# Sink-window attention by 64-query halves: 208 score columns per query, sinks inside the key slots

## The chip, the cores and the metric

One core of one Trainium2 chip runs the whole program. The metric is device time in microseconds for one execution. The engines that matter here are TensorE (matmuls and their weight loads), VectorE, ScalarE, GpSimd and SyncE, which only issues DMAs. Each engine works through its own queue in program order; a semaphore wait on one instruction holds up all that stand behind it on that engine.

## The reference

Input are q, k, v of shape (2, 8, 768, 64): two batches, eight heads, 768 positions, head width 64. Each query sees the keys of its own window (itself and the 127 before it) and the first `n_sink` keys (4 here, at most 16 in this path). Behind the attention come two feed-forward layers on 1536 tokens.

```
scores = q @ k^T / sqrt(64)
keep   = (key < n_sink) or (0 <= query - key < window)        # window = 128
a      = softmax(where(keep, scores, -1e9))
x      = (a @ v), heads side by side                          # 1536 x 512
x      = softplus(x @ w_in1) @ w_out1                         # 512 -> 2048 -> 512
out    = (h * clip(h + 3, 0, 6) / 6) @ w_out2,  h = x @ w_in2
```

## The kernel before

Attention works in groups: a group is one block of 128 queries with all eight heads, 12 groups (g = 0 to 11), six per batch; i = g mod 6 is the block within its batch. A half group n (0 to 23, two per group) is four heads. The loop at L623 runs over n and writes all engines' work in one fixed order, so that each engine's queue is the order of the text. `in_order` (L31) pins it: no planner moves anything within the attention.

For a half group, `scores` (L460 on in the text, matmul L483) multiplies q (64 rows of the head's width, 128 queries as weights) with 272 key columns: the block before and the own block, each in a slot of 128 keys and 8 sink columns of `ring`. The two heads of a pair lie in rows 0 to 63 and 64 to 127. Every head has a PSUM bank of its own. fp32 products show as two matmuls and two weight loads each. `exps` masks and takes the maximum on VectorE (L495), and the exponential with its sum on ScalarE (L500). `transposes` (L525) turns the probabilities, 128 x 128 at a time, by TensorE, and `copies` brings them from PSUM (L538 on VectorE, L540 on ScalarE). `apply_v` (L567) multiplies them with v, two blocks a head. The sinks' 16 columns go another way in blocks with i > 1: GpSimd collects the 64 sink columns of four heads (L505), one transpose (L516), one copy, and one product with the sinks' values, set up so that each head only meets its own (L552). Block i = 0 has 128 keys only, block i = 1 sees the sinks as ordinary keys.

Half n's second part (two heads) is transposed and applied in iteration n + 1, its first part transposed in iteration n and applied in n + 1. When a group's eight heads are complete, `normalise` (L581, VectorE) divides by the sum, `turn_x` (L589, TensorE) transposes the output, `store_hi` (L592, ScalarE) and `store_lo` (L596, VectorE) write it as a rounded part and its remainder; `store_lo` stands one iteration after `store_hi`.

Between, VectorE converts feed-forward weights (`Weights.half`, L96, L99, L102), then ScalarE (L106) and GpSimd (L107). `HALVES` (L26) says in which iterations: every odd one from 5 to 19, and each one from 20 to 23. DMA issues are on SyncE: `fetch` (q, k, v of a group, three groups ahead) and the weights.

The loop runs three iterations more than there are half groups. In the first two of these stand the first two products of the feed-forward part (`products`, L144, 12 matmuls each). Then the feed-forward part runs: `stage_a` (L144 and the activations L166 to L176), `stage_b` (L201), with the remaining 20 weight conversions under its first 16 steps.

Of the kernel before, what the change touches and what calls it, by code (L numbers as in the profile page):

```python
# [18 lines left out]
P = 128  # L19
NEG = 1.0e9  # L20
MAXSINK = 16
SK = MAXSINK // 2
SLOTW = P + SK
SLOTPOS = (0, 2, 1, 3)
# [343 lines left out]
def banded_attention(ctx, tc, qT_d, kT_d, v, ident, NSv, Wv, xT, psa, isq, w, ffn, flags):  # L368
# [8 lines left out]
    NS = 4 * MAXSINK  # L377
# [4 lines left out]
    pst = ctx.enter_context(tc.tile_pool(name="pst", bufs=2, space=PSUM))  # L382
    ps1 = ctx.enter_context(tc.tile_pool(name="ps1", bufs=1, space=PSUM))

    st = {}
    ring = one.tile([P, NP, 4, SLOTW], F32, name="ring")

    def fetch(g):
        b, i = divmod(g, NB)
        s = st.setdefault(g, {})  # L390
        s["q"] = thr.tile([P, NP, P], F32, tag="q", name=f"q_{g}")
        s["v"] = thr.tile([P, H, D], F32, tag="v", bufs=5, name=f"v_{g}")
        k = ring[:, :, SLOTPOS[g % 4], 0:P]

        for ps in (slice(0, NP),) if g else (slice(0, NP // 2), slice(NP // 2, NP)):
            for t, src, eng in ((s["q"], qT_d, nc.sync), (k, kT_d, nc.sync if g else nc.scalar)):
                src = src[b].rearrange("(p t) d s -> (t d) p s", t=2)[:, ps, i * P : (i + 1) * P]
                eng.dma_start(t[:, ps], src)
        nc.sync.dma_start(s["v"], v[b, i * P : (i + 1) * P])

    def fetch_sinks(b):

        t = two.tile([NS, H, D], F32, tag="vs", name=f"vs_{b}")
        rows = v[b, 0:MAXSINK].rearrange("m h d -> m (h d)")
        rows = bass.AP(rows.tensor, rows.offset, [[0, 4]] + [list(x) for x in rows.ap])
        nc.sync.dma_start(t.rearrange("p h d -> p (h d)"), rows)
        st["vs", b] = t

    def own_sinks(b):

        t = st["vs", b]
        nc.gpsimd.tensor_tensor(
            out=t, in0=t, in1=owner.rearrange("p (h o) -> p h o", o=1).to_broadcast([NS, H, D]), op=ALU.mult
        )
# [5 lines left out]
    wm = one.tile([P, 1], F32, name="wm")  # L420
    mA = one.tile([P, P], F32, name="mA")
    mB = one.tile([P, P], F32, name="mB")
    mS = one.tile([P, P], F32, name="mS")
    tB = one.tile([P, P], F32, name="tB")
    m_odd = one.tile([P, 2, SLOTW], F32, name="m_odd")
    m_even = one.tile([P, 2, SLOTW], F32, name="m_even")
    m_one = one.tile([P, 2, SLOTW], F32, name="m_one")
    m_zero = one.tile([P, P], F32, name="m_zero")
    ph = one.tile([NS, 2, 4], I32, name="ph")
    owner = one.tile([NS, H], F32, name="owner")  # L430

    def masks(i):

        if i == 0:
            nc.vector.tensor_scalar(out=mB, in0=rmc, scalar1=Wv, scalar2=hid, op0=ALU.is_ge, op1=ALU.mult)
            nc.vector.tensor_tensor(out=mB, in0=mB, in1=tB, op=ALU.min)
            nc.vector.tensor_scalar(out=mS, in0=col, scalar1=NSv, scalar2=None, op0=ALU.is_ge)
            nc.vector.tensor_tensor(out=m_zero, in0=mB, in1=mS, op=ALU.mult)
        elif i == 1:
            nc.vector.tensor_scalar(out=wm, in0=Wv, scalar1=-float(P), scalar2=None, op0=ALU.add)  # L440
            nc.vector.tensor_scalar(out=mA, in0=rmc, scalar1=wm, scalar2=hid, op0=ALU.is_ge, op1=ALU.mult)
            nc.vector.tensor_tensor(out=m_one[:, 0, 0:P], in0=mA, in1=mS, op=ALU.mult)
            nc.vector.tensor_copy(m_one[:, 1, 0:P], mB)
        else:
            m, j = (m_odd, 0) if i % 2 else (m_even, 1)
            nc.vector.tensor_copy(m[:, j, 0:P], mA)
            nc.vector.tensor_copy(m[:, 1 - j, 0:P], mB)
            nc.vector.tensor_scalar(
                out=m[:, :, P:SLOTW], in0=mS[:, 0:MAXSINK].rearrange("p (a c) -> p a c", a=2),
                scalar1=hid, scalar2=None, op0=ALU.mult,  # L450
            )

    def keep_sinks(g):
        b, i = divmod(g, NB)
        pos = SLOTPOS[g % 4]
        if i == 0:
            st["ks", b] = two.tile([P, NP, MAXSINK], F32, tag="ks", name=f"ks_{b}")
            nc.gpsimd.tensor_copy(st["ks", b], ring[:, :, pos, 0:MAXSINK])
        if i < 4:
            nc.gpsimd.tensor_copy(ring[:, :, pos, P:SLOTW], st["ks", b][:, :, (i % 2) * SK : (i % 2 + 1) * SK])  # L460

    def scores(n):
        g, quad = divmod(n, 2)
        i = g % NB
        s = st[g]
        if quad == 0:
            s["sum"] = two.tile([P, H], F32, tag="sum", name=f"sum_{g}")
            s["mx"] = two.tile([P, H], F32, tag="mx", name=f"mx_{g}")
        s["P", quad] = two.tile([P, 4, 2, SLOTW], F32, tag="P", bufs=2, name=f"P_{n}")
        s["s", quad] = []  # L470
        for p in range(quad * 2, quad * 2 + 2):

            for t in range(2):
                hh = len(s["s", quad])
                ps = (psa if hh < 3 else ps1).tile([P, 512], F32, tag="s" if hh < 3 else "s3", name=f"s_{n}_{hh}")
                rows = slice(t * D, (t + 1) * D)
                if i == 0:
                    rhs = ring[rows, p, SLOTPOS[g % 4], 0:P]
                else:
                    ee, oo = sorted((SLOTPOS[(g - 1) % 4], SLOTPOS[g % 4]))  # L480
                    rhs = ring[rows, p, ee : oo + 1 : oo - ee, :]
                ps = ps[:, 0 : P if i == 0 else 2 * SLOTW]
                nc.tensor.matmul(ps, s["q"][rows, p, :], rhs, start=True, stop=True)  # L483
                s["s", quad].append(ps)

    def exps(n, pair):
        g, quad = divmod(n, 2)
        i = g % NB
        s = st[g]
        w_ = P if i == 0 else 2 * SLOTW  # L490
        mask = m_zero if i == 0 else (m_one if i == 1 else m_odd if i % 2 else m_even).rearrange("p a c -> p (a c)")
        for hh in range(2 * pair, 2 * pair + 2):
            h = quad * 4 + hh
            xs = thr.tile([P, 2 * SLOTW], F32, tag="xs", bufs=4, name=f"xs_{n}_{hh}")[:, 0:w_]
            nc.vector.tensor_tensor_reduce(  # L495
                out=xs, in0=s["s", quad][hh], in1=mask, scale=-isq, scalar=3.0e38,
                op0=ALU.add, op1=ALU.min, accum_out=s["mx"][:, h : h + 1],
            )
            dst = s["P", quad][:, hh].rearrange("p a c -> p (a c)")[:, 0:w_]
            nc.scalar.activation(  # L500
                dst, xs, AF.Exp, scale=-1.0, bias=s["mx"][:, h : h + 1], accum_out=s["sum"][:, h : h + 1]
            )
        if i > 1 and pair == 1:
            s["PS", quad] = two.tile([P, 4, 2, SK], F32, tag="PS", name=f"PS_{n}")
            nc.gpsimd.tensor_copy(s["PS", quad], s["P", quad][:, :, :, P:SLOTW])  # L505

    def transposes(n, m):
# [5 lines left out]
        if m == 2:  # L513
            if i > 1:
                s["ps", m] = ps1.tile([P, 512], F32, tag="tr", name=f"pts_{n}")[0:NS, 0:P]
                nc.tensor.transpose(s["ps", m], s["PS", quad].rearrange("p h a c -> p (h a c)"), ident)  # L516
            return
        if i == 0:
            ins = [pt[:, hh].rearrange("p a c -> p (a c)")[:, 0:P] for hh in range(4)] if m else []
        else:  # L520
            ins = [pt[:, 2 * m + hh, j, 0:P] for hh in range(2) for j in range(2)]
        if ins:
            s["ps", m] = pst.tile([P, 512], F32, tag="pt", name=f"pt_{n}_{m}")
            for o, x in enumerate(ins):
                nc.tensor.transpose(s["ps", m][:, o * P : (o + 1) * P], x, ident)  # L525

    def copies(n, m):
        g, quad = divmod(n, 2)
        s = st[g]
        if ("ps", m) not in s:  # L530
            return
        ps = s.pop(("ps", m))
        if m == 2:
            t = two.tile([NS, P], F32, tag="PTS", name=f"PTS_{n}")
        else:
            t = two.tile([P, 512], F32, tag=f"PT{m}", name=f"PT_{n}_{m}")
        if m == 1:
            nc.vector.tensor_copy(t, ps)  # L538
        else:
            nc.scalar.activation(t, ps, AF.Copy)  # L540
        s["T", quad, m] = t

    def apply_v(n, m):
        g, quad = divmod(n, 2)
        b, i = divmod(g, NB)
        s = st[g]
        if "o" not in s:
            s["o"] = ps1.tile([P, H, D], F32, tag="o", name=f"o_{g}")
        if m == 2:
            if i > 1:  # L550
                hs = slice(quad * 4, quad * 4 + 4)
                nc.tensor.matmul(  # L552
                    s["o"][:, hs, :].rearrange("p h d -> p (h d)"), s["T", quad, 2],
# [242 lines left out]
```

## Time and profile before

| | us |
|---|---|
| median of 3 runs | 648.52 (647.56 to 648.88) |
| span of the profiled execution, first to last instruction | 646.4 |
| TensorE busy | 635.6 (98%) |
| TensorE weight loads busy | 523.0 (81%) |
| VectorE busy | 335.9 (52%) |
| ScalarE busy | 333.3 (52%) |
| GpSimd busy | 215.8 (33%) |

The profiled execution is known by its span; its own time isn't listed beside it. The median of the runs is 2.1 us above the span. TensorE's matmuls are pipelined and a record includes the time to the last result, so "busy" is more than the array's own work; what a row of matmuls costs is read from the chain of waits, which gives each piece the time until the next one takes over. The stages overlap: shares of the whole span say little about one of them.

### The profile page before, as it was taken

How to read it: one execution, taken by the hardware profiler on the slowest of the kernel's cores; microseconds unless marked ns; L12 is line 12 of the kernel's file. 1: busy time of each engine (PE TensorE's matmuls, PEld its weight loads, DVE VectorE, ACT ScalarE, POOL GpSimd, SP SyncE). 2: the span in 40 equal slices, each digit the busy share in tenths (PEclk: the TensorE clock that was granted, in tenths of full speed). 3: DMA queues.
4: the chain of work that ended last, by engine and by line, in shares of the span. 5: the costliest groups of instructions: out<-in, count | busy, mean ns of one | idle time of the engine just before them, and what ended most of it. 6: DMA issues, size and time to landing. Idle time of an engine off the chain costs nothing.

```text
span 646.4 us, 8792 instructions
## 1 busy us (share of the span) xinstructions
PE 635.6 (98%) x3148; PEld 523.0 (81%) x3148; DVE 335.9 (52%) x693; ACT 333.3 (52%) x707; POOL 215.8 (33%) x197
## 2 busy tenths in 40 slices
PE   8999999999999999999999999999999999999996
PEld 4898787878888888888888888888888888888884
DVE  4788989599922422225899987222232222322221
ACT  3777777578866756667777864222222222222221
POOL 1113123489964444445798964000000000000000
PEclk9999999999999999999999999999999999999999
DMA  7744572650000000004665731000010000100001
GB/s 205 236 135 144 164 243 81 233 209 1 1 1 1 0 2 1 1 7 132 189 193 171 219 100 34 1 1 0 2 65 1 0 1 1 65 1 0 1 1 70
DMA packets 38141, 47.06 MB, mean 73 GB/s; under 512 B 2120, under 2 KB 30792, under 8 KB 38088
## 3 DMA queue, kind: packets, MB, share of 16 engines
q1 hardware_dynamic: 37400, 46.15, 22.6%
q8 instruction: 26, 0.43, 0.3%
q10 hardware_dynamic: 688, 0.26, 0.2%
q14 instruction: 27, 0.22, 0.1%
HBM read 43.26 MB, written 3.15 MB: 72 GB/s over the span
## 4 chain that ended last, share of the span: by engine, by line
PE 88%; issue 5%; DVE 3%; ACT 2%; POOL 1%; POOLq 0%; ACTq 0%; DVEq 0%
PE y_w L201 39%; PE h_w L144 39%; PE o L567 3%; PE s L483 2%; PE pt L525 2%; PE spare L603 1%; PE o L552 1%; ACT P L500 1%; POOL w_w L107 1%; DVE xs L495 0%; PE xtr L589 0%; DVE t_w L102 0%; DVE e_w L174 0%; DVE PT L538 0%; POOL ring L460 0%
## 5 line engine op out<-in xcount | busy, mean ns | idle before, releaser
L144 PE MATMUL h_w<-xT,w_w 128*128 128x512 f32 x1152 | 281.9, 389 | 0.8 <-DVE e_w L174 0.8
L144 PEld LDWEIGHTS h_w<-xT,w_w 128*128 128x128 f32 x1152 | 215.9, 188 | 46.7 <-DVE e_w L174 1.3
L201 PE MATMUL y_w<-g_w,w_w 128*128 128x512 f32 x576 | 142.6, 389 | 0.0
L201 PE MATMUL y_w<-w_w,g_w 128*128 128x512 f32 x576 | 138.9, 389 | 0.0
L201 PEld LDWEIGHTS y_w<-w_w,g_w 128*128 128x128 f32 x576 | 108.0, 188 | 23.2 <-ACT g_w L181 0.4
L201 PEld LDWEIGHTS y_w<-g_w,w_w 128*128 128x128 f32 x576 | 108.1, 188 | 22.5
L107 POOL TENSOR_TENSOR w_w<-t_w,w_w 128x512 fp32r<-128x512 f32 x64 | 82.9, 1297 | 44.7 <-ACT w_w L106 44.3
L180 DVE SCALAR_TENSOR_TENSOR h_w<-e_w,h_w 128x512 f32<-128x512 f32 x48 | 33.4, 696 | 89.0 <-ACT e_w L178 89.0
L178 ACT ACTIVATE e_w<-h_w 128x512 f32<-128x512 f32 x48 | 28.7, 599 | 96.2 <-PE h_w L144 94.6
L176 POOL TENSOR_TENSOR g_w<-e_w,g_w 128x512 fp32r<-128x512 f32 x48 | 62.2, 1297 | 43.9 <-ACT g_w L175 43.9
L182 DVE SCALAR_TENSOR_TENSOR g_w<-h_w,g_w 128x512 fp32r<-128x512 f32 x48 | 33.2, 691 | 84.0 <-ACT g_w L181 84.0
L181 ACT ACTIVATE g_w<-h_w 128x512 fp32r<-128x512 f32 x48 | 28.7, 598 | 91.4 <-PE y_w L201 91.1
L170 POOL TENSOR_TENSOR u_w<-u_w,e_w 128x512 f32<-128x512 f32 x48 | 62.1, 1295 | 34.4 <-ACT u_w L169 33.6
L500 ACT ACTIVATE P<-xs,mx 128x272 f32<-128x272 f32 (+1 forms) x96 | 47.3, 494 | 31.8 <-DVE mx L495 31.7
L173 DVE SCALAR_TENSOR_TENSOR h_w<-h_w,r_w 128x512 f32<-128x512 f32 x48 | 33.4, 696 | 58.1 <-ACT r_w L171 58.1
L166 ACT ACTIVATE e_w<-h_w 128x512 f32<-128x512 f32 x48 | 28.4, 592 | 45.5 <-PE h_w L144 39.9
L174 DVE TENSOR_TENSOR e_w<-h_w,u_w 128x512 f32<-128x512 f32 x48 | 33.0, 688 | 28.8 <-POOL u_w L170 28.5
L567 PE MATMUL o<-v,PT 128*128 128x64 f32 x352 | 45.0, 271 | 1.5 <-DVE PT L538 1.3
L106 ACT ACTIVATE w_w<-t_w 128x512 fp32r<-128x512 f32 x64 | 40.0, 625 | 12.6 <-DVE t_w L102 11.7
L567 PEld LDWEIGHTS o<-v,PT 128*128 128x128 f32 x352 | 42.7, 191 | 3.0 <-DVE PT L538 1.9
L96 DVE TENSOR_SCALAR m_w<-raw_w 128x512 int32<-128x512 int32 x52 | 36.1, 693 | 7.5 <-DMA raw_w<-in_moe_w_in_dram 3.6
L175 ACT ACTIVATE g_w<-e_w 128x512 fp32r<-128x512 f32 x48 | 29.9, 624 | 17.4 <-DVE e_w L174 13.6
(80 smaller groups left out, 523.1 us busy)
## 6 DMA issues: line engine op xcount, KB each, us to landing
raw_w<-in_moe_w_in_dram SPq DMA_DIRECT2D x32, 512.0 KB, 5.1
raw_w<-in_moe_w_out_dram SPq DMA_DIRECT2D x32, 512.0 KB, 3.7
v<-in_v_dram SPq DMA_DIRECT2D x12, 256.0 KB, 5.3
out_dram<-o SPq DMA_DIRECT2D x12, 256.0 KB, 2.4
q<-in_q_dram SPq DMA_DIRECT2D x11, 256.0 KB, 3.0
ring<-in_k_dram SPq DMA_DIRECT2D x11, 256.0 KB, 3.8
ring<-in_k_dram ACTq DMA_DIRECT2D x2, 128.0 KB, 6.1
q<-in_q_dram SPq DMA_DIRECT2D x2, 128.0 KB
```

The lines of the kernel that those rows point to most:

```text
L96: nc.vector.tensor_scalar(out=m, in0=hi, scalar1=3, scalar2=0x3FFFFFF8, op0=ALU.logical_shift_left, op1=ALU.bitwise_and)
L106: nc.scalar.activation(wt[:, 0, :], t.bitcast(F32), AF.Copy)
L107: nc.gpsimd.tensor_tensor(out=wt[:, 1, :], in0=t.bitcast(F32), in1=wt[:, 0, :].bitcast(F32), op=ALU.subtract)
L144: nc.tensor.matmul(h, wt[:, ws, kk * P : (kk + 1) * P], xT[:, xs, kk, t0 : t0 + 512], start=(n == 0), stop=(n == 11),)
L170: nc.gpsimd.tensor_tensor(out=u, in0=u, in1=e, op=ALU.subtract)
L173: nc.vector.scalar_tensor_tensor(out=h, in0=h, scalar=0.0, in1=r, op0=ALU.max, op1=ALU.add)
L176: nc.gpsimd.tensor_tensor(out=glo, in0=e, in1=ghi.bitcast(F32), op=ALU.subtract)
L180: nc.vector.scalar_tensor_tensor(out=h, in0=e, scalar=6.0, in1=h, op0=ALU.min, op1=ALU.mult)
L182: nc.vector.scalar_tensor_tensor(out=glo, in0=h, scalar=1.0 / 6.0, in1=ghi.bitcast(F32), op0=ALU.mult, op1=ALU.subtract)
L201: ins = nc.tensor.matmul(y, lhsT, rhs, start=(c == 0 and n == 0), stop=(c == 15 and n == 2))
L500: nc.scalar.activation(dst, xs, AF.Exp, scale=-1.0, bias=s["mx"][:, h : h + 1], accum_out=s["sum"][:, h : h + 1])
L567: nc.tensor.matmul(s["o"][:, h, :], t[:, o : o + P], st[gg]["v"][:, h, :], start=(k == 0 and (i <= 1 or hh == 0)), stop=(k == len(blocks) ...
```

## The change

Each block of 128 queries is worked as two halves of 64. A half's queries see their own half block of keys and the two half blocks before it, 192 keys in place of 256, and the 16 sinks: 208 columns. `ring` goes; `keys` holds all six blocks of a batch, each slot as 64 keys, 16 sinks, 64 keys (144 columns), so that the columns a half needs are one run, or two. `spread_sinks` copies the 16 sinks into all slots once per batch (GpSimd). K is fetched by half blocks.

Scores of a pair of heads are now six matmuls on tiles of 64 rows by 64 columns: the first queries on 128 columns (part X) and 80 columns (part Y), the second on 208 columns at once. The heads of one parity of a half group share a PSUM tile of 512 columns (`s`, two tiles per half group instead of four). The sink columns are transposed with the Y part, 80 columns a head, so the separate sink transpose, copy and product go. The values are fetched in two forms: `vx`, 128 rows from the middle of the block before to the middle of this one, and `vy`, 80 rows (64 and the sinks) for each query half. `apply_x` is one product a head, `apply_y` two with 64 weight columns each. Both are moved one half group further back, to iteration n + 2. `normalise`, `turn_x`, `store_hi` and `store_lo` now all stand in the same even iteration; in it `store_lo` comes right behind `store_hi`. There are three PSUM tiles for transposes and two for the output. The mask for blocks with i > 1 is one (`m_gen`), made in the first iteration.

The core of the diff:

```diff
-SK = MAXSINK // 2
-SLOTW = P + SK
+HQ = P // 2
+SLOTW = P + MAXSINK
+YW = HQ + MAXSINK
+PW = P + YW
...
+    pst = ctx.enter_context(tc.tile_pool(name="pst", bufs=3, space=PSUM))
+    pso = ctx.enter_context(tc.tile_pool(name="pso", bufs=2, space=PSUM))
...
+    keys = one.tile([P, NP, NB, SLOTW], F32, name="keys")
...
+                    for r in range(2):
+                        c0 = r * (HQ + MAXSINK)
+                        eng.dma_start(keys[:, ps, i, c0 : c0 + HQ], src[:, :, r * HQ : (r + 1) * HQ])
+    def fetch_v(g):
...
+        nc.sync.dma_start(s["vx"], v[b, lo : lo + P])
+        if i:
+            s["vy"] = thr.tile([YW, 2, H, D], F32, tag="vy", name=f"vy_{g}")
+            lo = (i - 1) * P
+            nc.sync.dma_start(s["vy"][0:HQ, 0], v[b, lo : lo + HQ])
+            nc.sync.dma_start(s["vy"][HQ:YW, 0], v[b, 0:MAXSINK])
+            lo = i * P + HQ
+            nc.sync.dma_start(s["vy"][0:MAXSINK, 1], v[b, 0:MAXSINK])
+            nc.sync.dma_start(s["vy"][MAXSINK:YW, 1], v[b, lo : lo + HQ])
+    def spread_sinks():
+        nc.gpsimd.tensor_copy(
+            keys[:, :, :, HQ : HQ + MAXSINK],
+            keys[:, :, 0:1, 0:MAXSINK].to_broadcast([P, NP, NB, MAXSINK]),
+        )
...
+        s["s", quad] = [psa.tile([P, 2, 256], F32, tag="s", name=f"s_{n}_{t}") for t in range(2)]
+        for pp in range(2):
+            p = quad * 2 + pp
+            if i == 0:
+                parts = [None]
+            else:
+                parts = [(r0, HQ + MAXSINK, P, 0), (r1, HQ + MAXSINK, PW, 0), (r0, 0, YW, P)]
+            for part in parts:
+                for t in range(2):
...
+                        nc.tensor.matmul(
+                            ps[r, pp, at : at + n_], s["q"][rows, p, r],
+                            keys[rows, p].rearrange("p i c -> p (i c)")[:, lo : lo + n_], start=True, stop=True,
+                        )
...
+        for m, c0, rows in ((0, 0, P), (1, P, YW)) if i else ((0, 0, P),):
+            s["ps", m] = pst.tile([P, 512], F32, tag="pt", name=f"pt_{n}_{m}")
+            for hh in range(4):
+                nc.tensor.transpose(s["ps", m][0:rows, hh * P : (hh + 1) * P], pt[:, hh, c0 : c0 + rows], ident)
...
+    def apply_x(n):
...
+            nc.tensor.matmul(
+                s["o"][:, h, :], s["T", quad, 0][:, hh * P : (hh + 1) * P], s["vx"][:, h, :],
+                start=(hh == 0 or g % NB == 0), stop=(g % NB == 0),
+            )
+    def apply_y(n):
...
+            for j, r in enumerate((r0, r1)):
                 nc.tensor.matmul(
+                    s["o"][r, h, :], s["T", quad, 1][:, hh * P + j * HQ : hh * P + (j + 1) * HQ],
+                    s["vy"][:, j, h, :], start=False, stop=(hh == 3),
                 )
...
+        new, old, older = n < NQ, 0 <= n - 1 < NQ, 0 <= n - 2 < NQ
+        done = n // 2 - 2 if n % 2 == 0 and n >= 4 else None
         if new:
             scores(n)
+        elif n - NQ < 2:
+            ffn.products("w1", 0, n - NQ)
+        if done is not None:
             normalise(done)
...
+            exps(n, 0)
+            exps(n, 1)
         if old:
+            transposes(n - 1)
+            copies(n - 1)
         if new:
+            exps(n, 2)
+            exps(n, 3)
         if done is not None:
             turn_x(done)
+        if older:
+            apply_x(n - 2)
         if done is not None:
             store_hi(done)
+        if older:
+            apply_y(n - 2)
+        if n % 2 == 0 and n >= 2 and n // 2 - 1 < NG:
+            inverse(n // 2 - 1)
+        if done is not None:
+            store_lo(done)
+        if quad == 1 and new:
             if g % NB == 0:
+                spread_sinks()
+            if g + 2 < NG:
+                fetch_v(g + 2)
             if g + 3 < NG:
                 fetch(g + 3)
```

## Rows read from the trace of the kernel before

**Rows 1.** The page: its head and the busy times.
```profile
span 646.4 us, 8792 instructions
...
PE 635.6 (98%) x3148; PEld 523.0 (81%) x3148; DVE 335.9 (52%) x693; ACT 333.3 (52%) x707; POOL 215.8 (33%) x197
```

**Rows 2.** Busy time by stretch: start:end, length, engines (instructions), clock, DMA share, GB/s.
```profile
8.70:31.10 22.40, 21.27 (x166) 16.67 (x165) 17.28 (x78) 15.47 (x56) 2.55 (x6) 1.00 0.84 246
31.10:58.30 27.20, 27.16 (x220) 24.08 (x220) 22.03 (x75) 19.96 (x65) 5.40 (x10) 1.00 0.47 145
...
83.20:112.60 29.40, 29.00 (x223) 24.52 (x223) 25.79 (x82) 21.84 (x69) 8.66 (x11) 1.00 0.44 150
...
122.60:176.00 53.40, 52.57 (x232) 43.18 (x231) 50.46 (x78) 43.32 (x80) 46.92 (x38) 1.00 0.30 106
```

**Rows 3.** Chain of waits through one half group: start, us, engine, tile, line.
```profile
40.60 0.92 PE s L483 x7
41.52 0.59 PE pt L525 x4
42.10 0.11 PE pts L516
42.21 0.84 PE o L567 x8
43.05 0.44 PE pt L525 x4
43.50 0.88 PE o L567 x8
44.38 0.41 PE o L552
...
44.81 0.19 PE o L552
45.00 0.92 PE s L483 x7
```

**Rows 4.** The same chain in blocks i = 0 (first) and i = 1.
```profile
10.80 0.65 PE s L483 x8
...
17.65 1.12 PE s L483 x8
...
22.09 0.71 PE s L483 x4
```

**Rows 5.** Timeline of TensorE where the sink product meets the next scores.
```profile
39.90 0.48 PE L552 MATMUL o<-vs,PTS 64*128 64x256 f32 x1
39.92 0.49 PE L483 MATMUL s<-ring,q 64*128 64x272 f32 x1
40.22 0.38 PE L552 MATMUL o<-vs,PTS 64*128 64x256 f32 x1
```

**Rows 6.** Mask and maximum by shape: count, busy us, mean ns, idle before.
```profile
L495 DVE CUSTOM_DVE_ANT_0 xs<-s,m_odd 128x272 f32<-128x272 f32 x32 | 12.7, 435 | 3.4 <-PE s L483 2.0 <-ACT w_w L106 1.4
...
L495 DVE CUSTOM_DVE_ANT_0 xs<-s,m_zero 128x128 f32<-128x128 f32 x16 | 3.9, 286 | 2.1 <-PE s L483 2.1
```

**Rows 7.** Chain of waits where VectorE and ScalarE carry it.
```profile
90.83 0.35 DVE t_w L96
91.20 0.70 DVE t_w L99
...
94.09 0.60 DVE xT L596
...
95.29 0.35 DVE xs L495
...
99.14 1.13 ACT P L500 x4
```

**Rows 8.** Chain of waits at the seam to the feed-forward part.
```profile
112.64 2.99 PE h_w L144 x12
...
118.58 2.95 PE h_w L144 x12
121.53 0.45 PE xtr L589 x4
```

More of the change, by code (lines that the diff above doesn't have):

```diff
@@ L443, in masks @@
[L443 to L450, printed above, removed]
-            )
[L453 to L460, printed above, removed]
+            nc.vector.tensor_scalar(out=mt, in0=rel, scalar1=0.0, scalar2=hid, op0=ALU.is_lt, op1=ALU.mult)
@@ L489, in exps, with transposes @@
         s = st[g]
[L490 to L507, printed above, removed]
+        w_ = P if i == 0 else PW
+        mask = m_zero if i == 0 else m_one if i == 1 else m_gen
+        h = quad * 4 + hh
+        xs = thr.tile([P, PW], F32, tag="xs", bufs=4, name=f"xs_{n}_{hh}")[:, 0:w_]
+        nc.vector.tensor_tensor_reduce(
+            out=xs, in0=s["s", quad][hh % 2][:, hh // 2, 0:w_], in1=mask, scale=-isq, scalar=3.0e38,
+            op0=ALU.add, op1=ALU.min, accum_out=s["mx"][:, h : h + 1],
+        )
+        nc.scalar.activation(
+            s["P", quad][:, hh, 0:w_], xs, AF.Exp, scale=-1.0, bias=s["mx"][:, h : h + 1],
+            accum_out=s["sum"][:, h : h + 1],
+        )
+    def transposes(n):
         g, quad = divmod(n, 2)
@@ L512, in transposes @@
         pt = s["P", quad]
[L513 to L521, printed above, removed]
@@ L529, in copies @@
         s = st[g]
[L530 to L543, printed above, removed]
+        for m, rows in ((0, P), (1, YW)) if g % NB else ((0, P),):
+            t = two.tile([rows, 512], F32, tag=f"PT{m}", name=f"PT_{n}_{m}")
+            if m == 0:
+                nc.vector.tensor_copy(t, s["ps", m])
+            else:
+                nc.scalar.activation(t, s["ps", m][0:rows], AF.Copy)
+            s["T", quad, m] = t
@@ L557, in apply_v @@
-        for hh in range(2 * m, 2 * m + 2) if i else range(4 * m):
-            h = quad * 4 + hh
-            t = s["T", quad, m]
-            if i == 0:
-                blocks = [(hh * P, g)]
-            else:
-                o = (hh % 2) * 2 * P
-                first, second = (g - 1, g) if i % 2 else (g, g - 1)
-                blocks = [(o, first), (o + P, second)]
-            for k, (o, gg) in enumerate(blocks):
-                nc.tensor.matmul(
-                    s["o"][:, h, :], t[:, o : o + P], st[gg]["v"][:, h, :], start=(k == 0 and (i <= 1 or hh == 0)),
-                    stop=(k == len(blocks) - 1 and i <= 1),
+            s["o"] = pso.tile([P, H, D], F32, tag="o", name=f"o_{g}")
@@ L619, in banded_attention @@
     fetch(1)
[L620 removed]
+    fetch_v(0)
+    fetch_v(1)
     fetch(2)
[L622 removed]
+    nc.vector.tensor_scalar(out=rel[:, 0:P], in0=rmc, scalar1=float(HQ), scalar2=None, op0=ALU.add)
+    nc.vector.tensor_scalar(
+        out=rel[r0, P : P + HQ], in0=rmc[r0, 0:HQ], scalar1=float(P), scalar2=None, op0=ALU.add
+    )
+    nc.vector.memset(rel[r0, P + HQ : PW], 0.0)
+    nc.vector.memset(rel[r1, P : P + MAXSINK], 0.0)
+    nc.vector.tensor_scalar(
+        out=rel[r1, P + MAXSINK : PW], in0=rmc[r1, 0:HQ], scalar1=float(-HQ), scalar2=None, op0=ALU.add
+    )
     for n in range(NQ + 3):
         g, quad = divmod(n, 2)
[L625 to L626 removed]
+        new, old, older = n < NQ, 0 <= n - 1 < NQ, 0 <= n - 2 < NQ
+        done = n // 2 - 2 if n % 2 == 0 and n >= 4 else None
         if new:
             scores(n)
[L629 to L633 removed]
+        elif n - NQ < 2:
+            ffn.products("w1", 0, n - NQ)
+        if done is not None:
             normalise(done)
```

156 lines of the change are left out of this document (52 added, 104 removed).

## The prediction

> **What bounds the kernel now.** I read four views in this order. The page's head gives the span, 646.4 us, with TensorE busy 98% [rows 1]. A single busy figure hides the stages, so next comes the table by stretch [rows 2]: in 31.10 to 58.30 TensorE is busy 27.16 of 27.20 us, VectorE 22.03; the granted clock is 1.00, the upper of its two levels (2.4 GHz), in every stretch. Attention lasts to 112.6 us, then 53.4 us follow in which VectorE is the full engine (50.46 busy). The change touches attention and its seam to the feed-forward part only; whatever moves there moves everything after it by as much.
>
> Third, the chain of waits through one half group (one query block, four heads) [rows 3]: from 40.60 to 45.00 it stays on TensorE without a break, so a half group with neither of the two key-less blocks costs 4.40 us there: scores 0.92, transposes 0.59 and 0.44, the sink transpose 0.11, probabilities times values 0.84 and 0.88, sink product 0.41 and 0.19. Every second half carries the output's four transposes as well (0.45, [rows 8]), so a group is 2 x 4.40 + 0.4 = 9.2 us. Fourth, VectorE's own prices [rows 6, 7]: mask and maximum 0.35 a head at 272 columns (0.36 with its gap), a 128x512 pass 0.60, a weight conversion 0.35 + 0.70 + 0.70. Per group: 8 x 0.36 + 2 x 0.60 (copies) + 0.60 (normalise) + 0.60 (`store_lo`) + 1.75 = 7.0. The stretch itself says 22.03 / 27.20 x 9.2 = 7.45; the 0.4 between is the small sum and reciprocal of `inverse`. So TensorE leads VectorE by 1.7 us a group. That is all the change can win before VectorE takes over.
>
> **The change, TensorE side, one half of a block with i >= 2.**
> Scores: 4 matmul pairs on 272 columns become 12 on 128, 208 and 80. The eight old matmuls run as two streams, one per 64-row half of the array: a sink matmul of the upper half waits from 39.90 to 40.22 while a score matmul begins between, at 39.92 [rows 5]. So a stream does four in 0.92, 0.23 for 272 columns, and 208 columns cost 0.175. If the two column halves (queries 0-63 and 64-127) overlap as the row halves do, each of the four tiles has 4 x 208 columns: 0.70. If they don't, 1.40. No row has two column halves in flight; I take 0.70, because the row halves show that separate parts of the array don't queue for each other. Saved 0.22 (other end: lost 0.48).
> The Trainium skill, "TensorEngine Tiling (Array Packing)", Key Properties, has tiles independent, which speaks for 0.70; the same section says that changing the tiling mode drains the engine, and the new kernel goes 128x128, 128x64, 64x64 in each half. The trace shows a price for a row change (next sentences) and none for 128 to 64 columns; by the rule one more drain would add 0.17 a half, 0.34 a group, which VectorE's limit below would still cover.
> Row switch: scores behind the sink product, already in the 64-row mode, take 0.92, behind a 128-row product 1.12 with eight matmuls [rows 4], so 0.17 to 0.20 of the old 0.41 is the switch. The sink product's 0.60 goes and 0.17 stays: saved 0.43. The sink transpose, 0.11, goes; it stood between 128-column work without a gap, so 64-column loads beside 128-column ones cost no switch there.
> Values: 16 matmuls (0.84 + 0.88) become 8: saved 0.88. Added: 16 with 64 weight columns on the Y part. The old ones cost 0.105 each although only 64 columns stream, as long as a transpose with 128 (0.11), so their 128-column load sets the pace; 64-column loads go at half, 0.056, together 0.90. Bounds: 0.45 if the two column halves overlap, 1.68 if each costs the old 0.105. I take 0.90, the nearest by columns loaded. The eight transposes stay eight (four on 80 columns, kept at 0.11).
> Sum: 4.40 - 0.22 - 0.43 - 0.11 - 0.88 + 0.90 = 3.66; a group 7.72.
> Blocks with i = 1 had no sink product: 17.65 to 22.09 less 0.44 is 4.0 [rows 4], now 3.66, 0.33 saved each. Blocks with i = 0 lose: each 128-column score becomes two of 64 with the full weight load, 16 instead of 8 matmuls; they took 0.65 [rows 4], the pitch of the load, so +0.43.
>
> **VectorE and ScalarE side.** 64 columns fewer: (435 - 286) / 144 = 1.03 ns a column [rows 6], so 0.066 a head off 0.36, 0.295. Per group VectorE has 7.4 - 0.5 = 6.9 of work, but its order now costs a wait. In an even half it does `normalise`, two masks, the copy, two masks, then `inverse`, then `store_lo`, which needs ScalarE's `store_hi`; and that is queued behind four exponentials and a copy. Two exponentials took 1.13 [rows 7], some 0.5 each at 208 columns: 0.5 until the first can start + 2.0 + 0.6 + 0.6 = 3.7 us after the scores end, so `store_lo` ends at 4.3, while VectorE's masks and copy were through at 1.8. Before, `store_lo` stood an iteration later, with its data long there. Odd half: 1.78 + 1.75 (conversion), and 0.60 for the next `normalise`: 4.1. Loop: 8.4 a group, above TensorE's 7.72. So VectorE sets the pace and a group saves 9.2 - 8.4 = 0.8, not 1.5.
> The other new wait: heads of one parity now share a PSUM tile, so the first mask may have to wait for all scores. At worst 0.35 later each half, at best nothing; it moves the 8.4 within 8.1 to 8.8. The Trainium skill, "PSUM — Partial Sum Buffer", section "PSUM bank collisions raise a hardware error", wants accesses guarded by bank; by it the wait is there, and no row of this kernel has two engines in one bank at once.
>
> **Sum over attention.** Six groups (2 to 5, 8, 9): 6 x 0.8 = 4.8. Groups 10 and 11 convert in each half, VectorE-bound already (25.79 of 29.40 busy, [rows 2]): they gain the shorter masks, some 0.4 each, 0.8. Blocks 0 and 1, twice: 4 x 0.33 - 4 x 0.43 = -0.4. In the start (8.70 to 31.10) TensorE is idle 22.40 - 21.27 = 1.1 us behind copies and exponentials; products two halves behind take those waits away: 1.1 (against it some 1 us more mask set-up on VectorE; ends 0 and 1.1). Together 6.3.
>
> **The tail gives back.** From 112.64 to the end of the last output transposes TensorE took 9.3 us, the two feed-forward products (2.99, 2.95) inside [rows 8]. One half deeper, it does there: 2.99, transposes 1.03, output 0.45, X and Y 0.84 + 0.90, 2.95, X and Y again 1.74, then an uncovered wait for `normalise` (0.6 of work and 0.4 of latency), 0.45, and 0.2 of switches: 12.5. ScalarE's next activations and VectorE's conversions stand behind it. Lost 3.2; net 6.3 - 3.2 = 3.1.
>
> **Nearly free.** The values' DMAs grow (X, and Y's overlapping rows with the sinks), K comes in 256-byte pieces; the share of the DMA engines is 0.47 in 31.10 to 58.30, and each block is fetched three groups ahead, so I cost them at 0; with that cover gone in the start, 1 us. Eight DMA issues a group on SyncE have 8 us. The sinks' spreading is one GpSimd copy per batch, ahead of the second block: 0, or 1 us once if it waits for the queue of early loads. GpSimd's and ScalarE's small sink copies go; neither set the pace.
>
> The time shown is 648.52, the profiled span 646.4, so 2.1 lies around it; 646.4 - 3.1 + 2.1 = 645.4.
>
> **Rivals.**
> *Column halves don't overlap* (slower): scores 1.40, half 4.37. Six groups gain 0, four i = 1 halves lose 0.37 each, i = 0 loses 1.7, the start gains 1.1, the tail loses 3.2: +5, 653.5. For it: no row shows the overlap. Against: two row halves do. It decides as soon as scores take over some 1.0.
> *The instruction stream binds*: a half now has 112 loads and matmuls instead of 70. The densest stretch is 16 in 0.65 us [rows 4], 0.041 each; at that 4.6 a half: 657. Against: that stretch is explained by its columns.
> *Waits eat it*: the bank wait in full and `store_lo` later still, 9.0 a group: 648.
> *VectorE's wait doesn't bite*: TensorE's 7.72 holds, 6 x 0.7 more: 641.3.
>
> **How the numbers follow.** Forecast 0.45, VectorE free 0.15, waits 0.13, no overlap 0.18, instruction stream 0.09. About 0.2% (1.3 us) can be told from no change. Faster 0.60, same 0.13, slower 0.27. The forecast's own range is 643 to 647; with the other cases down to 640.5 and up to 653.5, which leaves out the instruction stream and a little on either side.
>
> **What would show it.** Right: score matmuls of both query halves overlapping, some 0.9 from first load to first transpose; Y products at 0.056; group period 8.4; VectorE waiting for ScalarE's `store_hi`; first feed-forward product near 106 us and last output transposes 12 to 13 us after it. Wrong: scores of 1.4, a period over 9, or a tail that costs nothing.

## The result

The changed kernel takes 638.20 us (median of 4 runs, 637.95 to 639.20), the kernel before 648.04 in the same comparison: ratio 0.9854, 95% interval 0.9840 to 0.9868. That is 9.8 us faster where 3.1 was forecast, and below the range's lower end of 640.5.

The head of the page and the table by stretch, of the changed kernel, answer to [rows 1, 2]:

```profile
span 636.5 us, 9690 instructions
...
PE 619.1 (97%) x3612; PEld 513.0 (81%) x3612; DVE 329.5 (52%) x693; ACT 324.9 (51%) x691; POOL 206.5 (32%) x170
```

```profile
7.85:26.00 18.15, 17.33 (x235) 14.73 (x234) 13.95 (x73) 12.29 (x49) 0.43 (x1) 1.00 0.93 274
26.00:49.80 23.80, 22.29 (x352) 19.98 (x348) 20.07 (x74) 17.24 (x60) 3.83 (x3) 1.00 0.88 227
...
73.20:99.40 26.20, 22.85 (x350) 20.12 (x348) 22.33 (x74) 17.08 (x57) 5.09 (x4) 1.00 0.66 201
112.10:166.00 53.90, 53.05 (x235) 43.58 (x234) 50.26 (x78) 43.11 (x79) 45.50 (x36) 1.00 0.25 89
```

The stretches hold the same iterations as those of before (0 to 5, 6 to 11, 18 to the first feed-forward product, and a piece of the feed-forward part with 78 VectorE instructions in both). Three groups take 23.80 in place of 27.20, and TensorE, full there before, now has 1.5 us of idle time. The start is down from 22.40 to 18.15, and there TensorE's own busy time fell by 4 us. The feed-forward stretch takes about as long as before (53.40 and 53.90).

The chain of waits through one group of blocks with i >= 2, which answers to [rows 3]; columns: start, us, what:

```profile
33.69 0.93 PE s L487 x14
34.63 0.53 PE pt L518 x3
...
35.21 0.38 issue
35.59 0.70 DVE x L565
...
36.33 0.66 PE xtr L573 x4
36.99 0.84 PE o L538 x8
37.83 0.61 PE o L551 x16
38.44 0.86 PE s L487 x20
39.30 1.03 PE pt L518 x8
40.33 0.84 PE o L538 x8
41.17 0.62 PE o L551 x16
41.79 0.25 PE s L487
```

The odd half (from 38.44) is TensorE's alone: 0.86 + 1.03 + 0.84 + 0.62 = 3.35. The even one leaves TensorE: its output transposes wait for `normalise` (L565). Together 8.10 a group.

To see where the time went, the start of the first score matmul of chosen half groups, read from TensorE's timeline and counted from the first score of each trace. (That first score itself came at 8.69 in the trace of before and 7.84 in that of after; over the thirteen traces of the changed kernel and its variants it lies between 7.38 and 8.95 although nothing ahead of it differs among them, so the 0.85 us between these two says nothing of the change. Without it the change is worth 9.0 us in these two traces, which is what the rows below add up to.)

| at the start of | before | after | gained in the stretch | forecast for it |
|---|---|---|---|---|
| iteration 2 | 5.16 | 4.16 | 1.00 | -0.86 |
| iteration 6 | 22.45 | 18.18 | 3.27 | 2.56 |
| iteration 12 | 49.63 | 41.96 | 3.40 | 2.4 |
| iteration 16 | 65.42 | 56.36 | 1.39 | -0.2 |
| iteration 20 | 83.30 | 73.43 | 0.81 | 1.6 |
| first feed-forward product | 103.88 | 91.58 | 2.43 | 0.8 |
| end of the last output transposes | 113.27 | 104.27 | -3.30 | -3.2 |

So the tail gives back what was forecast, to 0.1 us. Groups 3 to 5 (the third row) are 1.0 better. The error is at the starts of both batches (1.9, 0.7 and 1.6 us in the first, second and fourth row) and ahead of the feed-forward part (1.6); groups 8 and 9 of the second batch fall 0.8 short.

### The profile page after: what moved, and what is told of

The parts are those of the page before. It is cut to its first block, busy times and chain, and to the rows that moved or that the text cites. A ratio compares the mean times of both kernels' runs of the same rounds, so it can differ in the third digit from the quotient of the medians.

```text
span 636.5 us, 9690 instructions
## 1 busy us (share of the span) xinstructions
PE 619.1 (97%) x3612; PEld 513.0 (81%) x3612; DVE 329.5 (52%) x693; ACT 324.9 (51%) x691; POOL 206.5 (32%) x170
## 4 chain that ended last, share of the span: by engine, by line
PE 90%; DVE 5%; issue 2%; ACT 2%; DMA 1%; SPq 0%; DVEq 0%; ACTq 0%
PE y_w L202 40%; PE h_w L145 39%; PE o L538 3%; PE s L487 2%; PE pt L518 2%; PE o L551 2%; DVE x L565 1%; PE spare L587 1%; PE xtr L573 1%; DVE xs L500 1%; DMA raw_w<-in_moe_w_in_dram 1%; PE s L480 1%; DVE t_w L100 0%; DVE PT L526 0%; DVE t_w L103 0%
## 5 line engine op out<-in xcount | busy, mean ns | idle before, releaser
L504 ACT ACTIVATE P<-xs,mx 128x208 f32<-128x208 f32 (+1 forms) x96 | 42.8, 447 | 21.9 <-DVE mx L500 21.8
L103 DVE SCALAR_TENSOR_TENSOR t_w<-raw_w,m_w 128x512 int32<-128x512 int32 x52 | 35.5, 683 | 2.7
L100 DVE SCALAR_TENSOR_TENSOR m_w<-raw_w,m_w 128x512 int32<-128x512 int32 x52 | 35.9, 691 | 1.1
```

What stands on the lines that cost most here:

```text
L100: nc.vector.scalar_tensor_tensor(out=m, in0=hi, scalar=-0x40000000, in1=m, op0=ALU.bitwise_and, op1=ALU.bitwise_or)
L103: nc.vector.scalar_tensor_tensor(out=t, in0=lo, scalar=29, in1=m, op0=ALU.logical_shift_right, op1=ALU.bitwise_or)
L504: nc.scalar.activation(s["P", quad][:, hh, 0:w_], xs, AF.Exp, scale=-1.0, bias=s["mx"][:, h : h + 1], accum_out=s["sum"][:, h : h + 1],)
```

## The experiments

Each is an edit of the changed kernel, timed in five rounds (four to twelve runs) beside the kernel before. The diffs show the core of each edit. Differences "against the changed kernel" are between medians.

**e1: what if the Y products cost what the forecast put in?**

```diff
-            for j, r in enumerate((r0, r1)):
+            for k, r in enumerate((r0, r1, r0, r1)):
+                j = k % 2
...
```

> Each product of the Y part is issued twice (so Y is counted twice in the output; only the time is read). The 16 products with their row switch then take some 1.07 us in place of 0.61 in each half with i > 0, which is about the price that the prediction had put in. Theory A, VectorE sets the pace of the steady groups (2 to 5, 8 to 11) and TensorE that of the start, of the seam between the batches and of the tail: the 0.46 counts in some 8 to 10 halves, +3.5 to +4.5 us, and the group period between 26 and 50 us stays at 8.1. Rival B, TensorE sets the pace everywhere: 20 x 0.46 = +9 us, period 9.0. Rival C, TensorE nowhere sets it: under +1 us.

Measured 640.24, +2.0; ratio to before 0.9882 (0.9868 to 0.9897). Its chain from the same place:

```profile
33.54 1.08 PE o L552 x32
34.62 0.86 PE s L487 x20
35.48 1.03 PE pt L518 x8
36.51 0.44 PE xtr L574 x4
36.94 0.84 PE o L538 x8
37.78 1.08 PE o L552 x32
...
41.59 1.08 PE o L552 x32
```

Sixteen more matmuls cost 1.08 - 0.61 = 0.47. If the first sixteen cost as much, the change from 128 x 128 to 80 x 64 tiles costs the other 0.14. The period stays at 8.05 (33.54 to 41.59), now all TensorE: the two engines' loops are then equally long. By the 2.0 us the 0.47 counts in some four halves of 20, where 8 to 10 were expected. Theory A is right in kind; TensorE leads in fewer halves than it says.

**e2: is VectorE in the loop that sets the steady pace?**

```diff
...
             exps(n, 3)
+            nc.vector.tensor_tensor(out=pad, in0=rel, in1=mt if n else rel, op=ALU.min)
```

> One more VectorE instruction of 128 x 208 behind the masks of each half group (24 in all, some 0.28 us each; its output is not used). Theory A, VectorE paces the steady groups: the period grows by 0.5, over 8 groups +4 us, and nothing in the TensorE-paced start, so +4 to +5 in all. Rival B, TensorE paces: 0 to +1 us, since the pad fits into VectorE's idle 1.1 us a group.

Measured 641.77, +3.6; 0.9909 (0.9895 to 0.9922). Counted from the first score, the start of each odd iteration from 7 to 21 falls 0.28 to 0.31 further behind the changed kernel, and the start of an even one by nothing more. So VectorE paces: an odd iteration's pad delays the next `normalise`, for which TensorE waits. In an even iteration the pad vanishes in VectorE's wait for `store_hi`. That is theory A at some 0.3 a group, where 0.5 was expected. Another 0.45 comes in iteration 22; there the trace has the lower clock from 94 to 97 us.

**e3: the depth undone.**

```diff
-        if older:
-            apply_x(n - 2)
+        if old:
+            apply_x(n - 1)
...
-        if older:
-            apply_y(n - 2)
+        if old:
+            apply_y(n - 1)
```

> Only the depth is undone: the X and Y products of half n stand in iteration n + 1, as in the kernel before, with the output work left where it is. Theory D, the depth is one shift with two ends, that is, what the tail loses (X and Y of one half, 1.5 us, past the feed-forward products) the start had won by not having that work yet: 0, within 1.5 us. Rival E, the depth removes waits in each iteration for the copies of the transposed probabilities: +4 us or more, and TensorE waits for PT in each half (some 0.2 to 0.5). Rival F, the prediction's own view, the depth only costs a tail: -1.5 to -3 us.

Measured 645.29 (643.72 to 648.72), +7.1; 0.9972 (0.9954 to 0.9991). This is the run that decides: without its depth the change is worth 2.5 us against the kernel before of the same rounds, not 9.8. TensorE waits for the copied probabilities (waits by line, 8 to 110 us; total, times, longest; the changed kernel has no such row):

```profile
PE o L538 <- DVE PT L526: 10.0, 14, 2.1
```

Something comes on top. The table by stretch of e3:

```profile
92.00:94.00 2.00, 0.57 (x6) 0.31 (x3) 1.95 (x7) 0.53 (x1) 0.00 (x0) 1.00 0.93 324
94.00:96.00 2.00, 1.32 (x17) 1.26 (x19) 1.97 (x9) 2.00 (x9) 1.27 (x1) 1.00 0.07 19
...
98.00:100.00 2.00, 2.00 (x12) 1.91 (x11) 1.82 (x11) 1.65 (x6) 1.19 (x1) 0.50 0.00 0
...
104.00:106.00 2.00, 0.91 (x8) 0.91 (x8) 2.00 (x10) 2.00 (x7) 1.27 (x1) 1.00 0.83 289
...
108.00:110.00 2.00, 2.00 (x7) 1.52 (x6) 0.19 (x1) 0.26 (x1) 1.27 (x1) 0.50 0.96 361
```

After gaps (0.57 and 1.32 busy of 2.00 us, later 0.91) the granted clock falls to 0.50, the lower level (1.2 GHz), twice; eight transposes then take 1.93 in place of 1.03 and the twelve matmuls of the first feed-forward product 4.55 in place of 2.97. The four runs whose mean clock is 0.999 took 643.7 to 643.9, the eight with 0.994 or 0.991 took 645.1 to 648.7. So the depth is worth 5.6 us at a kept clock, and the rest of the 7.1 goes with the clock. Theory E, with fewer and longer waits than one in each half, and with the clock beside it; D and F fall.

**e4: `store_lo` one iteration later.**

```diff
+        if n % 2 == 1 and n >= 5:
+            store_lo(n // 2 - 2)
...
-        if done is not None:
-            store_lo(done)
+        if n == NQ + 2:
+            store_lo(NG - 1)
```

> store_lo moves from right behind store_hi to the next iteration, behind its first two masks; all else as in the changed kernel. Theory A, VectorE's wait for store_hi (11 waits, 12.6 us in all) is in the loop that sets the pace: up to 0.5 to 0.6 a group goes before TensorE's own 7.5 binds, -4 to -5 us, period 7.5 to 7.6 between 26 and 50 us. Rival B, the wait is slack beside TensorE: 0, within 0.7 us, and the idle time shows up in front of another VectorE instruction.

Measured 636.91, -1.3; 0.9829 (0.9816 to 0.9842). The period between iterations 8 and 12 is 8.06, as in the changed kernel (8.09), so A falls for the steady groups. The gain is in the last groups, which have a conversion in each half: counted from the first score, 1.4 us in iteration 22 and 1.1 in the tail, less 0.4 lost in iteration 6. VectorE has the same hole, in front of the next mask. Of the two fences the first is the changed kernel, the second e4 (timeline of VectorE; start, us; at the end the idle time before):

```profile
38.16 0.20 DVE L560 RECIPROCAL rs<-rs 128x8 f32<-128x8 f32 x1
39.50 0.69 DVE L580 TENSOR_TENSOR xT<-xtr,xT 128x512 fp32r<-128x512 f32 x1 [1.14 <-ACT xT L576]
40.11 0.36 DVE L500 CUSTOM_DVE_ANT_0 xs<-s,m_gen 128x208 f32<-128x208 f32 x1
```

```profile
39.30 0.20 DVE L560 RECIPROCAL rs<-rs 128x8 f32<-128x8 f32 x1
40.61 0.38 DVE L500 CUSTOM_DVE_ANT_0 xs<-s,m_gen 128x208 f32<-128x208 f32 x1 [1.11 <-ACT xT L576]
```

The release that the view names in the second is ScalarE's, but that mask reads the scores, whose last matmul ends at 40.43 in e4's chain.

**e12: the output's transposes behind the Y products, `store_lo` left in its place.**

```diff
-        if done is not None:
-            turn_x(done)
         if older:
             apply_x(n - 2)
-        if done is not None:
-            store_hi(done)
         if older:
             apply_y(n - 2)
+        if done is not None:
+            turn_x(done)
+            store_hi(done)
```

> Only turn_x and store_hi go behind apply_y; store_lo stays right behind store_hi, as in the changed kernel. Theory M, the steady period of 8.1 us is the length of two loops at once: one over normalise and TensorE's X, Y and scores, one over ScalarE's exponentials, store_hi and VectorE's wait in store_lo. With the first cut alone the second still binds (store_lo ends where it ended, the four masks, the copy, the conversion and normalise follow): period 8.0 to 8.1, 638.2 within 0.7 us. Rival P, the loop over normalise alone set the pace, and e5 owed nothing to store_lo: period 7.6, 634.3 to 635.5.

Measured 639.04 (637.93 to 642.61), no change that can be told; 0.9880 (0.9855 to 0.9906). The period is 8.06 (iterations 8 to 12), as M has it, and P falls. The chain now runs over ScalarE, from the masks back to the masks:

```profile
36.27 0.28 DVE xs L500
...
36.59 1.01 ACT P L504 x4
37.61 0.48 ACT PT L528
38.09 0.90 ACT P L504 x4
38.99 0.49 ACT xT L576
...
40.11 0.36 DVE xs L500
```

**e5: both.**

> store_lo in the next iteration, as in e4, and turn_x with store_hi behind apply_y instead of ahead of apply_x. Theory L, the steady period of 8.1 us is a loop over two engines: from turn_x, which waits for normalise, over TensorE's X, Y and next scores (2.97 us with the transposes of the output) to VectorE's masks, copy and conversion and the next normalise. Then X, Y and the scores no longer stand behind normalise, the loop is cut, and the period falls to the larger of TensorE's own 7.5 and VectorE's 7.0: 7.5, -0.5 in some 9 groups, -4 to -5 us against the changed kernel. Rival V, VectorE alone sets 8.1 by its work and its wait for ScalarE: 0, within 1 us of e4 (636.9).

Measured 634.85, -3.4; 0.9797 (0.9784 to 0.9809). The period is 7.58, the chain never leaves TensorE, and in two groups it has no idle time (chain, then table by stretch):

```profile
33.92 0.90 PE s L487 x16
34.83 1.05 PE pt L518 x8
35.88 0.84 PE o L538 x8
36.72 0.61 PE o L551 x16
37.34 0.59 PE xtr L573 x4
37.92 1.07 PE s L487 x13
```

```profile
33.85:49.01 15.16, 15.16 (x236) 13.73 (x233) 13.69 (x51) 11.92 (x41) 2.55 (x2) 1.00 0.84 242
```

So the 8.1 of the changed kernel is the length of two loops at once. One goes from `normalise` over TensorE's X, Y and next scores to the masks, the conversion and the next `normalise`; the other from the masks over ScalarE's exponentials and `store_hi` to `store_lo` and the next masks. Each edit alone cuts one (8.06 twice); only both reach 7.58, TensorE's own time in this order. Theory L, at 3.4 of its 4 to 5 us; V falls. The order has a price on TensorE: its output transposes, between Y and the scores, take 0.59 and the scores behind them 1.07, where e1's chain, with the transposes ahead of X, has 0.44 and 0.86. Without its doubled Y that chain is 8.05 - 2 x 0.47 = 7.1.

The first feed-forward product, counted from the first score, is then 4.3 us earlier, of which the tail takes 0.8 back: TensorE waits there 2.2 us (105.4 to 107.6) for a `normalise` queued on VectorE behind an activation. Behind that wait the clock is at its lower level until 111 us; four transposes take 1.12 and the next product 3.79. All five runs show a mean clock of 0.994 or 0.995.

**e6: the depth undone at the start alone.** Halves 0 to 5 are applied at n + 1, the others at n + 2.

> Halves 0 to 5 are multiplied with the values one iteration behind their scores, as in the kernel before; from half 6 on two behind (iteration 7 has no product with the values). Theory S, the start is where the depth wins: the sixth half's scores come 3.5 us later (1.9 by iteration 2, where the work of half 0 was not yet due, 1.6 for waits on the copies), and next to nothing of it comes back in iteration 7, because the groups there go at the pace of the loop over VectorE: +2.5 to +3.5 us in all, tail and clock as in the changed kernel. Rival T, what the start wins is given back at once in the steady groups: +0.5 us or less.

Measured 641.07, +2.9; 0.9896 (0.9882 to 0.9911). Counted from the first score, iteration 2 starts 1.9 us later than in the changed kernel and iteration 6 3.5; iteration 7, which has no products with values, gives 1.45 back (X 0.84, Y 0.61), and iteration 8 half of that is lost again; from iteration 9 to 22 the distance stays within 0.1 of 2.7. The trace has the lower clock from 94 to 97 us, in iteration 22; at the end of the last output transposes the distance is 2.7 again, so the 2.9 is not the clock's. Theory S. The chain of e6 in iteration 1 shows the price, TensorE behind VectorE's copy:

```profile
12.23 0.69 DVE PT L526
...
12.97 1.10 PE o L538 x8
14.08 0.86 PE s L487 x20
```

In the changed kernel the scores of iteration 2 start at 12.00, ahead of that copy.

**e7 and e9: the depth undone at the end alone,** halves 18 to 23 at n + 1; in e9 with five spare matmuls in the gaps.

> The other end: halves 18 to 23 one iteration behind (iteration 19 has the products of 17 and 18). Theory S: the tail is 1.5 us shorter, because X and Y of half 23 no longer stand behind the first feed-forward products, but the first of these products starts 1 to 2 us later: 0 within 1 us, if the granted clock stays at its upper level. Rival K, the clock: TensorE's gaps in these iterations (it waits for the copies of the probabilities behind VectorE's conversions) bring the granted clock to its lower level for some 2 to 4 us before and in the first feed-forward products, as in e3 between 97 and 100 and between 107 and 111 us: +1 to +3 us, and the times of the runs spread over 2 us or more.

> As e7 (halves 18 to 23 one iteration behind), with five spare bf16 matmuls of 512 columns (some 0.22 us each, results unused) ahead of the X products in iterations 19 to 24, where TensorE had stood idle for 1 to 1.4 us each time. Theory K, the gaps bring the clock down: no stretch at the lower level between 90 and 115 us, all runs within 1 us of each other at 639.5 to 640.5. Rival: the gaps are not what brings it down: the runs spread over 639.5 to 645 as those of e7.

e7 took 643.49 (639.53 to 645.11), ratio 0.9931 (0.9907 to 0.9955); its profiled execution kept the upper clock and took 639.53, +1.3. There the first product starts 3.4 us later, counted from the first score (1 to 2 was expected), and the tail is 1.7 shorter. The two runs with a mean clock of 0.999 took 639.5 and 639.6, two with 0.994 took 643.2 and 643.8, two with 0.991 took 644.8 and 645.1: theory K, larger than expected. In e9 no 2 us stretch of the trace between 90 and 115 us is below the upper level, and all five runs show 0.997 or 0.998: 641.36 (641.10 to 642.49), 0.9908 (0.9894 to 0.9921). The runs lie 1.4 apart where 1 was expected, and the spare matmuls cost 1.8 over e7's best, more than expected; they still win 2.1 on its median.

**e8: the second feed-forward product behind the last X and Y.**

> The second feed-forward product of the loop stands behind the X and Y products of the last half instead of ahead of them. Theory N, in the changed kernel the last normalise and its output (0.70 and the wait around it, 1.4 us from the last Y product to the first output transpose's successor) lie bare on the path: they are now covered by 3.0 us of products, -0.7 to -1.3 us. Rival O, ScalarE's activations behind the two products set the end there: 0 within 0.4 us.

Measured 638.09, no change that can be told; 0.9849 (0.9836 to 0.9862). In the trace the last output transposes end 0.8 us earlier, counted from the first score, and so does TensorE's last matmul (622.0 in place of 622.8): N's size. The medians keep 0.1, O's size, with runs of one kernel 0.9 to 1.3 apart. Between the two it stays open.

**e10: e5, with the end of the loop in another order.** The last `normalise` stands ahead of the second product, and the first product's activation behind both.

```diff
...
+        if n == NQ + 1:
+            normalise(NG - 1)
+            ffn.products("w1", 0, 1)
...
-        if n == NQ:
+        if n == NQ + 1:
             ffn.activate("w1", "softplus", 0, 0, lambda: None)
```

> As e5, and at the end of the loop: the second feed-forward product stands behind the X and Y products of the last half, the last normalise right behind those in front of the product, and the activation of the first product after it. Theory N, in e5 the last output transposes wait for normalise, which stands on VectorE behind the activation's e_w, itself held by GpSimd (5.6 us from 101.2 to 107.6 without TensorE work, with the lower clock behind it from 106 to 112 us): that gap goes, the last output transposes end some 11 us behind the first product's start in place of 13.5, and the clock stays up: -2.5 to -3.5 us against e5 (634.85), that is 631.3 to 632.4. Rival O, ScalarE's activations set what follows: 0 to -1 us.

Measured 633.31 (632.33 to 634.25); 0.9775 (0.9762 to 0.9789): 1.5 us below e5, the best of all, 14.3 below the kernel before. That is short of N's 2.5 to 3.5 and above O's 1. TensorE has no gap from 95 to 107 us, and the last transposes end 10.8 us behind the first product's start, as expected:

```profile
95.00:107.00 12.00, 12.00 (x112) 10.45 (x111) 8.86 (x22) 7.76 (x18) 3.85 (x3) 1.00 0.88 303
```

The clock stays at its upper level until the last 2 us of the trace, so part of the 1.5 is the clock that e5 lost behind its wait. (TensorE stood idle 2.2 us in e5's gap, not the 5.6 of the expectation: there the chain had only left TensorE.) Some 1 us is lost again behind that, where a product waits 1.7 us for VectorE's e_w (0.8 in the changed kernel).

**e11: two conversions from the last groups to the seam between the batches** (`HALVES` with 12 and 14 in place of 20 and 22).

> As e10, with two of the twelve weight conversions moved from iterations 20 and 22 to 12 and 14, the first groups of the second batch, whose masks are short. Theory A, VectorE paces the last two groups (15.85 of 16.19 us busy in e5, against 15.16 for two steady groups): these fall to the steady period, -1.0 us, and the seam has 1.4 us of VectorE time left for each conversion of 1.75, +0.3 to +0.6: -0.4 to -0.8 in all. Rival: the conversions cost the seam as much as they cost the end: 0 within 0.3 us.

Measured 635.26 (634.46 to 638.12), 0.9820 (0.9800 to 0.9840), 2.0 slower than e10: neither the expected gain nor the rival's 0. Against e10 its trace loses 1.9 us from iteration 14 to 18 and wins 1.0 in iteration 22: the seam had less to spare than its busy time let expect. The two traces end 0.9 apart. The other 1.1 of the medians is not explained; e10's profiled execution, 634.25, is the slowest of its five, and three of e11's five show a mean clock of 0.990 or 0.997.

## Why the prediction was wrong

**The step that failed is the depth.** The prediction gave it 1.1 us ("products two halves behind take those waits away: 1.1") and charged X and Y of one half, 1.74, to the tail: -0.6 in all. The runs give it +5.6 at a kept clock (e3), +7.1 by the medians. Of the 5.6, 2.9 lie at the start (e6) and 1.3 at the end (e7); the 1.4 that is left belongs by subtraction to the middle. No run has it alone, but e3's trace shows the place: counted from the first score, it is behind the changed kernel by 3.5 us at iteration 6, 4.2 at 12, 6.0 at 16 and 5.2 at 20, so most of it is at the start of the second batch.

Two errors are in that one step. First, the shift was charged at its late end and not credited at its early one. The sum went by half groups, each with its own scores, transposes and products; but time goes by iterations, and in iterations 0 to 5 the new order has X and Y of halves 0 to 3 only. The 1.45 that e6 gets back in iteration 7 is this credit, measured. As e3 does the same matmuls as the changed kernel, charge and credit cancel in it, and its 5.6 is what waiting costs on balance. Second, 1.1 was TensorE's idle time in the start of the kernel before [rows 2], taken as the most that a depth can win. The idle time of the old order said nothing of the waits that the new order would have without its depth: 10.0 us in front of X (e3). Why the old order had fewer is read from its text and not tested: it transposed the first two heads of a half in the half's own iteration, between the products of other heads; the new one gave that up, and its depth stands in its place.

**The rest of the sum held, as a total and by stretch.** Without the two depth terms it was 6.3 - 1.1 - (3.2 - 1.74) = 3.7; e3's runs at the upper clock are 3.9 below before. In the rows of the table above, e3's trace stands against that sum so:

| at the start of | e3 gains in the stretch | forecast without depth |
|---|---|---|
| iteration 2 | -0.9 | -0.9 |
| iteration 6 | 1.6 | 1.5 |
| iteration 12 | 2.7 | 2.4 |
| iteration 16 | -0.4 | -0.2 |
| iteration 20 | 1.6 | 1.6 |
| first feed-forward product | 0.3 | 0.8 |
| end of the last output transposes | -3.2 | -1.5 |

The last two rows carry e3's lower clock: 0.9 us in the transposes, 1.6 in the product. Inside the stretches some of the agreement is luck, as the next paragraphs show: Y was priced too high and VectorE's loop too long, and e3's waits were not in the sum. The extra PSUM tiles stay in e3, so their worth is in the 3.9; no run takes them away. And one term put at nothing was not quite nothing: in the kernel before, the weight loads of the scores waited 0.9 us in two times, at iterations 6 and 18, for GpSimd's copy to `ring` (L460).

**Scores, right.** 0.70 and a switch of 0.17 were put in; the chain has 0.86 to 0.93 for both. The four tiles of 64 x 64 get their weights at once (one line of the changed kernel, 38.37 to 38.40 us; min/median/max ns):

```profile
L487 PEld LDWEIGHTS s<-keys,q x4: 129/129/129, 38.4 to 38.4; 64*64 64x64 f32 x4
```

Four loads of 129 ns begin within 30 ns. "TensorEngine Tiling (Array Packing)" of the Trainium skill, Key Properties, has tiles independent, and the trace now agrees for columns too. The rival of the halves that don't overlap, 0.18, is out.

**Y products, half the price.** 0.90 was put in, 0.47 plus a switch of 0.14 measured (e1), the low bound of 0.45, for the same reason as the scores. The argument that columns don't queue was used for the scores and not for Y. The drain on a change of tiling, which the Trainium skill has in the same section and the prediction weighed at 0.17 a half and left out, shows here as some 0.14. Together a TensorE half is 3.35, not 3.66; by e1's 2.0 us for 0.47 a half that is worth some 1.3 us in all, since it counts only where TensorE leads.

**VectorE sets the pace, right; the wait behind it, half right.** Forecast 8.4 a group with `store_lo` behind `store_hi`, measured 8.1, and e2 shows VectorE in the loop. But taking that wait away moves nothing (e4), as a second loop over `normalise` and `turn_x` is as long (e12, e5). The prediction followed one loop and stopped. The wait for the shared score tile, priced at 0 to 0.35 a half, is there in e4, whose mask starts 0.18 us behind the last score matmul; no run takes it away.

**Block 0.** It was charged 0.43 for each half with sixteen loads instead of eight. Sixteen take 1.05 in the chain (0.65 before [rows 4]), so the price was right. In the first block iteration 0 pays it (2.49 us in place of 2.05) and iteration 1 more than returns it, because it has no product with values to wait for (1.67 in place of 3.12).

**The tail, right in total:** 12.5 us forecast from the first feed-forward product to the last output transposes, 12.7 measured:

```profile
106.23 2.97 PE h_w L145 x12
109.20 0.84 PE o L538 x8
110.04 0.64 PE o L551 x16
...
110.70 0.70 DVE x L565
...
111.45 0.67 PE xtr L573 x4
```

The bare `normalise` between Y and xtr is the one that was named: TensorE idles 0.8 us for it, where 1.0 was put in. The match to 0.2 is partly luck. X and Y stand there twice, and Y is each time some 0.3 cheaper than its price; against that TensorE waits 0.7 us for the `normalise` of the group before, behind VectorE's last conversion (ahead of 104.12), which was not in the sum. The first product came at 99.4, not 106, because of all that is above.

## What to carry over

A pipeline made deeper has two ends: whoever charges the drain has to credit the fill, and the sum is best made by iterations (what work is due in each) rather than by pieces of work. The idle time of the old order bounds what a change of order wins only if the old order's other covers stay. When a wait is found in a loop, look for a second loop of about the same length before pricing its removal: here each cure alone won nothing in the steady groups, and both together 0.5 us a group.

## What was not expected of the hardware

TensorE's clock fell in some executions of one program and not in others. e7's six runs, one kernel on one chip, have mean clocks from 0.999 to 0.991 and times from 639.5 to 645.1. In e3 two falls are in the trace, behind stretches in which TensorE was 0.57 and 0.91 busy of 2.00 us. The profiled executions of e2 and e6 have one too (94 to 97 us), and that of e5 (107 to 111). Such a gap alone does not decide: the changed kernel's trace has TensorE 0.74 busy from 90 to 92 us and 1.40 in the next 2 us, e7's 0.88 and 1.01 from 88 to 92, and both stay at the upper level there. With five spare matmuls per iteration in the gaps, e9's trace has no fall between 90 and 115 us, and none of its five runs shows a mean clock below 0.997. What decides between runs stays open. In e12 two of six runs show it too (0.987, 642.4 and 642.6), though its profiled execution does not.

The mean clock has to be read with care: in every trace here the last microseconds (up to 5), behind TensorE's last matmul, are at the lower level as well. In the changed kernel's trace that is all there is (from 632 us on, the last matmul ends at 630.7), and its mean is 0.997.
